# Late expert slots of one and a half blocks in place of two, with the two halves of the split in one matmul

## The chip, the core and the metric

The kernel runs on one core of one Trainium2 chip, as one program. The metric is the device time of one execution in microseconds. Before the change three runs gave 578.73, 578.89 and 579.51 us, so the median is 578.89 us.

## The reference, cut to what matters

The computation is an attention with a small memory, followed by a mixture of experts. The part that the change touches is the second one, for 4608 tokens of 512 numbers, 8 experts and 1024 hidden units:

```python
logits = x @ w_gate                      # x: 4608 x 512, from the attention
e_idx = np.argmax(logits, axis=1)        # one expert per token
probs = softmax(logits); gate_w = probs[arange(N), e_idx]
eom = 1.0 / (1.0 + np.exp(-(x @ w_output_gate)))
for e in range(8):
    mask = e_idx == e
    if not mask.any():
        continue
    h = np.maximum(x[mask] @ w1[e], 0.0)  # 512 -> 1024
    ye = h @ w2[e]                        # 1024 -> 512
    out[mask] = gate_w[mask, None] * eom[mask, e, None] * ye
```

With the inputs of this case the reference sends 576, 576, 0, 0, 576, 1152, 1152 and 576 tokens to the eight experts. These counts come from running the reference's routing, not from the trace.

## The kernel before, in words

The first 120 us belong mostly to the attention. It writes rows of `x` with their gate factor to a buffer `xs` in device memory, and the routing (`rank`, `route_early`, `route_late`) works out lists of token numbers for *slots*. A slot is one pass of one expert's 4 MB of weights over a fixed number of token blocks of 128. There are 5 early slots of three blocks, filled as soon as enough tokens are known, then 5 late slots of three (`NPT`), 4 late slots of two (`NPP`, below called pairs), and 22 single slots behind a branch, which run only if something is left over. `route_late` counts blocks per expert (`nbi`, L346 to L351), takes away triples, then makes a pair of every remainder of two blocks (L360), and leaves the rest to single slots. With the counts above, four experts have a remainder of two blocks, in each of which only 192 of the 256 places hold a token; no single slot runs.

The arithmetic keeps fp32 accuracy by splitting each operand into a first part (a cast to fp32r) and a second part (what the cast left over). A product is the sum of three matmuls: first x first, second x first, first x second (`PASS`). The layout of one slot, in `several`:

- Layer 1 has four steps `u`, each with one 512 KB piece of `w1`. In each of two halves `j` and four chunks `cc` of the 512 inputs there are three matmuls of moving width 128 times the number of blocks (L1176). The result stands in a PSUM bank; ScalarE writes `relu` of it as the first part `hh` (L1181), VectorE writes the second part `hl` (L1182). For a pair both halves share one bank and one such evacuation; for a triple each half has its own.
- Layer 2 has four steps `u` with pieces of `w2`, for each block `k` six matmuls of moving width 512 (L1198). After the last one `finish_y` scales the block with the gate on ScalarE (L1155) and scatters it to `out` with GpSimd (L1156). A result tile `y` has two buffers.

Each piece of weights is loaded by the SP queue (L553), cast by ScalarE (L564) and its second part subtracted by VectorE (L565). That is `split`; the finished halves go to a ring of ten places (`ring`, 2 + 2 + 6, grown by `GROW`). `done`, called after each step, moves the ring on: it issues at most two splits, and no more than nine pieces ahead of use (`ring.size - 1`), so that in the steady state each step issues exactly one. The tokens of a slot are gathered from `xs` by GpSimd, up to three slots ahead; for the slots behind the first late one (`quart`) this is done in quarters of 32 tokens, four indirect DMAs for each block (L519). `turn_x` then transposes a chunk on VectorE (L1035), casts it on ScalarE (L1043) and subtracts on VectorE (L1044). It is called for the four chunks of the *next* slot during layer 2 of the current one (`TURN`).

The order is written out by hand: every engine executes its instructions in the order in which the program lists them, and engines wait for each other by semaphores. What ScalarE and VectorE find in their queues during a slot is therefore this, in this order: in layer 1, for each `u`, the evacuations and then one split (cast, subtraction); in layer 2 the `turn_x` chunks of the next slot with the splits between them; and `finish_y` behind the chunks. The PSUM pool of this stage has six banks that are used in turn.

Of the kernel before, what the change touches and what calls it, by code (L numbers as in the profile page):

```python
# [16 lines left out]
P = 128  # L17
# [49 lines left out]
def attention_moe(tc, phiT, kv, qT, wgo, wall, out):  # L67
# [3 lines left out]
    with contextlib.ExitStack() as ctx:  # L71
# [266 lines left out]
        def route_late():  # L338
# [4 lines left out]
            yield from hold(LATE["dve"])  # L343
            epc = epcs[-1]
            nbi = rt.tile([P, E], I32, name="nbi", bufs=1)
            V.tensor_scalar(nbi[:], n_, 127.0, None, ALU.add)  # L346
            taken.clear()
            yield
            V.tensor_scalar(nbi[:], nbi[:], 7, None, ALU.arith_shift_right)
# [8 lines left out]
            V.tensor_tensor(ti[:, 2], nbi[:], ti[:, 0], ALU.subtract)  # L358
            yield
            V.tensor_scalar(ti[:, 1], ti[:, 2], 2.0, 2.0, ALU.is_ge, ALU.mult)  # L360
            yield
            V.tensor_tensor(ti[:, 2], ti[:, 2], ti[:, 1], ALU.subtract)
            yield
# [134 lines left out]
        for s in range(NSLOT):  # L498
# [4 lines left out]
            else:  # L503
# [3 lines left out]
            slots.append({"s": s, "nb": nb, "q0": q0, "idx": idx[nm], "rows": rows,  # L507
                          "nm": nm, "quart": s not in WHOLE,
                          "known": False, "listed": False})
        order = slots  # L510

        def gather(z):
            z["xg"] = xgs.tile()
            for k in range(z["nb"]):
                q = z["q0"] + k
                if z["quart"]:
                    rows = 4 * z["rows"]
                    for b in range(4):
                        G.indirect_dma_start(  # L519
                            out=z["xg"][:, k, XQ * b:XQ * b + XQ], out_offset=None,  # L520
                            in_=xs[0:z["rows"]].rearrange("t (a q) -> (t a) q", a=4),
                            in_offset=bass.IndirectOffsetOnAxis(ap=z["idx"][2][:, b, q:q + 1], axis=0),
                            bounds_check=rows - 1, oob_is_err=False)
                    continue
                G.indirect_dma_start(
                    out=z["xg"][:, k], out_offset=None, in_=xs[0:z["rows"]],
                    in_offset=bass.IndirectOffsetOnAxis(ap=z["idx"][0][:, q:q + 1], axis=0),
                    bounds_check=z["rows"] - 1, oob_is_err=False)
# [492 lines left out]
        def turn_x(z, c):  # L1021


            nb, xg = z["nb"], z["xg"]
            n = nb * P
            if c == 0:
                z["x"] = (mo.tile([P, 4, 3 * P], F32R, name="xh"), mo.tile([P, 4, 3 * P], F32R, name="xl"))
                if z["quart"]:
                    z["g"] = env["xt"].tile([P, 3], F32, name="gx")
                    for b in range(4):  # L1030
                        A.copy(z["g"][32 * b:32 * b + 32, 0:nb], xg[0:32, 0:nb, XQ * b + P])
            xh, xl = z["x"]
            if z["quart"]:
                xt = env["xt"].tile([P, 3 * P], F32, name="xt")
                V.transpose(xt[:, 0:n].rearrange("p (k i) -> p k i", i=32),  # L1035
                            xg[:, 0:nb].rearrange("p k (b q) -> p (k b) q", b=4)[:, :, 32 * c:32 * c + 32])
                pt = xt[:, 0:n]
            else:
                pt = bank([512], "ps")
                for k in range(nb):  # L1040
                    T.transpose(pt[:, k * P:(k + 1) * P], xg[:, k, c * XQ:c * XQ + P], ident[:])
                pt = pt[:, 0:n]
            A.copy(xh[:, c, 0:n], pt)  # L1043
            V.tensor_tensor(xl[:, c, 0:n], pt, xh[:, c, 0:n].bitcast(F32), ALU.subtract)  # L1044

        NT = 5 * NBP
        deferred = []
# [104 lines left out]

        def finish_y(z, k, py):
            y = mo.tile([P, DM], F32, name="y", bufs=2)
            A.activation(y[:], py, AF.Copy, scale=z["g"][:, k:k + 1] if z["quart"] else z["xg"][:, k, P:P + 1])  # L1155
            G.indirect_dma_start(  # L1156
                out=out, out_offset=bass.IndirectOffsetOnAxis(ap=z["idx"][1][:, z["q0"] + k:z["q0"] + k + 1], axis=0),
                in_=y[:], in_offset=None, bounds_check=NTOK - 1, oob_is_err=False)

        def several(i, st, nxt, hook):  # L1160

            z = order[i]
            nb, x, h = z["nb"], z["x"], []
            n_ = nb * P
            for u in range(4):
                w = st.take(i, u)
                h_ = mo.tile([P, 2, 3 * P], F32R, name="hh", bufs=4)
                l_ = mo.tile([P, 2, 3 * P], F32R, name="hl", bufs=4)
                for j in range(2):
                    if nb == 3 or j == 0:  # L1170
                        pb = bank([1, 512] if nb == 3 else [2, 256], "ps")
                    n = 0
                    for cc in range(4):
                        for a, b in PASS:
                            o = cc * 256 + j * P
                            T.matmul(pb[:, j % pb.shape[1], 0:n_], w[:, b, o:o + P], x[a][:, cc, 0:n_],  # L1176
                                     start=(n == 0), stop=(n == 11))
                            n += 1
                    if nb == 3 or j == 1:
                        js = slice(j, j + 1) if nb == 3 else slice(0, 2)  # L1180
                        A.activation(h_[:, js, 0:n_], pb[:, :, 0:n_], AF.Relu)  # L1181
                        V.scalar_tensor_tensor(l_[:, js, 0:n_], pb[:, :, 0:n_], 0.0, h_[:, js, 0:n_].bitcast(F32),  # L1182
                                               ALU.max, ALU.subtract)
# [6 lines left out]

            turns = [(u, k) for u in range(4, 8) for k in range(nb)]
            if 8 * i + 8 == st.hi:
                turns.sort(key=lambda t: t[1])
            for step, (u, k) in enumerate(turns):
                w = st.take(i, u)
                for f in range(2):
                    for n, (a, b) in enumerate(PASS):
                        T.matmul(py[k], h[u - 4][a][:, f, k * P:(k + 1) * P], w[:, b, DM * f:DM * f + DM],  # L1198
                                 start=(u == 4 and f == 0 and n == 0), stop=(u == 7 and f == 1 and n == 2))
# [5 lines left out]
                if k == nb - 1:  # L1205
                    st.done(PUMP[0])

        def single(i, st, nxt):
# [157 lines left out]
```

## Time and profile before

| | us |
|---|---|
| median of three runs | 578.89 |
| time of the profiled execution | 577.36 |
| span of the profiled execution | 575.6 |
| TensorE matmul busy | 529.1 (92%) |
| VectorE busy | 356.1 (62%) |
| ScalarE busy | 280.4 (49%) |
| GpSimd busy | 229.2 (40%) |
| mean granted clock | 0.966 |

The late slots stand at the end of the span. By the timeline the last four late triples start at 345.1, 378.0, 411.1 and 444.1 us, the four pairs at 477.1, 499.5, 522.0 and 544.4 us, and the last matmul starts at 566.6 us. The columns of the profile are busy time, number of instructions, and mean nanoseconds of one. Matmuls overlap in it: the mean length of one is its latency, and the distance between two starts is what it costs.

### The profile page before, as it was taken

The numbers are of one execution on the slowest core, as the hardware profiler recorded it, in microseconds if no ns is written. First come the engines' busy times: TensorE is split into PE (matmuls) and PEld (weight loads), VectorE is DVE, ScalarE is ACT, GpSimd is POOL, SyncE is SP. The second block draws the span as 40 slices with busy tenths as digits, with TensorE's granted clock in tenths as the row PEclk, the third lists the DMA queues.
The fourth block names the chain that finished last, engine by engine and source line by source line (L and its number), as shares of the span: only waits on it lengthen the run. The fifth ranks groups of instructions, "written<-read, shape, count | busy, mean of one in ns | idle before, by whom it ended". The sixth has DMA issues, their size and how long they took to land. (4 is left out here: it accounts for less than half of the span.)

```text
span 575.6 us, 10886 instructions
## 1 busy us (share of the span) xinstructions
PE 529.1 (92%) x4031; PEld 455.6 (79%) x4031; DVE 356.1 (62%) x736; ACT 280.4 (49%) x496; POOL 229.2 (40%) x253
## 2 busy tenths in 40 slices
PE   3688886789899999999999999999999999999993
PEld 2455554478689799898998989898998989899893
DVE  4485979767765659996443555646465555676610
ACT  3475655454254456453434545445454445656510
POOL 2242575831166034312471735547170604553011
PEclk9987879989899999999999999999999999999998
DMA  8999999975367659756564665656465655687000
GB/s 308 413 401 391 382 376 356 308 301 168 116 197 245 209 173 308 246 155 183 161 200 145 204 177 180 184 171 176 139 202 168 179 172 181 198 264 223 7 28 32
DMA packets 42238, 124.14 MB, mean 216 GB/s; under 512 B 10368, under 2 KB 10432, under 8 KB 41792
## 3 DMA queue, kind: packets, MB, share of 16 engines
q1 hardware_dynamic: 35136, 102.71, 54.7%
q0 software_dynamic: 7040, 20.65, 10.4%
q8 instruction: 33, 0.54, 0.4%
q14 instruction: 29, 0.24, 0.1%
HBM read 102.99 MB, written 20.87 MB: 215 GB/s over the span
## 5 line engine op out<-in xcount | busy, mean ns | idle before, releaser
L1176 PE MATMUL bps<-xh,whl 128*128 128x384 f32 (+1 forms) x896 | 213.6, 322 | 0.1
L1198 PE MATMUL bps<-whl,hh 128*128 128x512 f32 x608 | 197.7, 396 | 0.0
L565 DVE TENSOR_TENSOR whl<-w,whl 128x1024 fp32r<-128x1024 f32 x112 | 136.8, 1228 | 68.5 <-ACT whl L564 68.5
L1176 PEld LDWEIGHTS bps<-xh,whl 128*128 128x128 f32 x896 | 156.9, 190 | 1.9 <-issue 0.6
L1176 PE MATMUL bps<-xl,whl 128*128 128x384 f32 (+1 forms) x448 | 143.8, 321 | 0.0
L1198 PEld LDWEIGHTS bps<-whl,hh 128*128 128x128 f32 x608 | 114.7, 189 | 26.1 <-issue 2.5
L1198 PE MATMUL bps<-whl,hl 128*128 128x512 f32 x304 | 119.0, 391 | 0.0
L564 ACT CAST whl<-w 128x1024 fp32r<-128x1024 f32 x112 | 116.4, 1046 | 0.0
L519 POOL DMA_INDIRECT xg<-xs,idx_ql x80 | 90.2, 1127 | 25.2 <-issue 24.3
L1181 ACT ACTIVATE hh<-bps 128x384 fp32r<-128x384 f32 (+1 forms) x96 | 48.9, 510 | 96.9 <-PE bps L1176 96.7
L1182 DVE SCALAR_TENSOR_TENSOR hl<-bps,hh 128x384 fp32r<-128x384 f32 (+1 forms) x96 | 55.1, 577 | 52.1 <-ACT hh L1181 52.1
L1176 PEld LDWEIGHTS bps<-xl,whl 128*128 128x128 f32 x448 | 85.1, 190 | 0.5
L1156 POOL DMA_INDIRECT out<-y,idx_ol x23 | 24.9, 1081 | 127.1 <-ACT y L1155 101.4
L1198 PEld LDWEIGHTS bps<-whl,hl 128*128 128x128 f32 x304 | 57.5, 189 | 10.8
L838 POOL TENSOR_TENSOR ea<-ea,mx 128x512 f32<-128x512 f32 (+1 forms) x20 | 19.2, 961 | 49.8 <-DVE mx L836 45.4
L1043 ACT CAST xh<-xt 128x384 fp32r<-128x384 f32 (+1 forms) x32 | 14.7, 460 | 37.9 <-DVE xt L1035 37.9
L873 ACT COPY xo<-bpd 128x576 f32<-128x576 f32 x36 | 22.6, 640 | 21.3 <-PE bpd L871 12.7
L956 POOL TENSOR_SCALAR Aw<-iota_row,row 128x128 bf16<-128x128 bf16 x36 | 26.8, 759 | 12.4 <-DVE row L946 12.4
L871 PE MATMUL bpd<-ve_b,aT 64*128 64x144 f32 (+1 forms) x320 | 28.5, 327 | 2.4 <-DVE ea L833 2.4
L1044 DVE TENSOR_TENSOR xl<-xt,xh 128x384 fp32r<-128x384 f32 (+1 forms) x32 | 15.8, 492 | 24.1 <-ACT xh L1043 24.1
L1155 ACT ACTIVATE y<-bps,gx 128x512 f32<-128x512 f32 x20 | 13.4, 687 | 30.4 <-PE bps L1198 13.9
L871 PEld LDWEIGHTS bpd<-ve_b,aT 64*128 64x128 f32 (+1 forms) x320 | 21.7, 196 | 8.1 <-issue 3.5
(248 smaller groups left out, 471.6 us busy)
## 6 DMA issues: line engine op xcount, KB each, us to landing
w<-wall SPq DMA_DIRECT2D x112, 512.0 KB, 3.9
kvt<-kv SPq DMA_DIRECT2D x32, 512.0 KB, 7.5
xs<-xo SPq DMA_DIRECT2D x16, 576.0 KB, 5.8
qt<-qT SPq DMA_DIRECT2D x16, 512.0 KB, 9.1
ph<-phiT SPq DMA_DIRECT2D x3, 1152.0 KB, 12.1
kv<-kv SPq DMA_DIRECT2D x4, 512.0 KB, 9.0
xg<-xs,idx_ql POOLq DMA_INDIRECT x80, 4.2
ph<-phiT SPq DMA_DIRECT2D x4, 288.0 KB, 3.2
```

What stands on the lines that cost most here:

```text
L519: G.indirect_dma_start(out=z["xg"][:, k, XQ * b:XQ * b + XQ], out_offset=None, in_=xs[0:z["rows"]].rearrange("t (a q) -> (t a) q", a=4), i ...
L564: A.copy(hl[:, 0], w[:])
L565: V.tensor_tensor(hl[:, 1], w[:], hl[:, 0].bitcast(F32), ALU.subtract)
L838: G.tensor_tensor(eav, eav, mx[:, 0:n].unsqueeze(2).to_broadcast([P, n, M]), ALU.subtract)
L871: T.matmul(px[to:to + n, r, sl], z["aT"][h, o:o + n], ves[2 * bp + b][h, g], start=True, stop=True)
L873: A.copy(xo[:, c % 2], px[:, :, 0:2 * XQ])
L956: (G if AWP else V).tensor_scalar(Aw[:, bp * NCH + c], iota_row[:], row[:, c:c + 1], None, ALU.is_equal)
L1156: G.indirect_dma_start(out=out, out_offset=bass.IndirectOffsetOnAxis(ap=z["idx"][1][:, z["q0"] + k:z["q0"] + k + 1], axis=0), in_=y[:], in ...
L1176: T.matmul(pb[:, j % pb.shape[1], 0:n_], w[:, b, o:o + P], x[a][:, cc, 0:n_], start=(n == 0), stop=(n == 11))
L1181: A.activation(h_[:, js, 0:n_], pb[:, :, 0:n_], AF.Relu)
L1182: V.scalar_tensor_tensor(l_[:, js, 0:n_], pb[:, :, 0:n_], 0.0, h_[:, js, 0:n_].bitcast(F32), ALU.max, ALU.subtract)
L1198: T.matmul(py[k], h[u - 4][a][:, f, k * P:(k + 1) * P], w[:, b, DM * f:DM * f + DM], start=(u == 4 and f == 0 and n == 0), stop=(u == 7 an ...
```

## The change

The four pairs become slots of one and a half blocks, 192 tokens, and stand between the triples.

- Routing: a flag `odd` says whether the expert's number of half blocks is odd. Only a remainder of two blocks whose second is at most half full becomes a pair. Three VectorE instructions on 128 x 8 numbers are added, with one more step in the routing's generator.
- `x` of a pair: first and second part lie next to each other in one tile of 384 columns. The second block is gathered with two indirect DMAs in place of four, and `turn_x` works on 192 columns.
- Layer 1 of a pair: for each `j` and `cc` one matmul with the first part of the weights over all 384 columns, and one with the second part over 256 columns, in place of three over 256. Each `j` now has a bank of its own. The two sums of columns have to be added: ScalarE copies the second 192 columns out of PSUM, VectorE adds the first, ScalarE writes `relu`, VectorE subtracts twice (64 and 128 columns), so that first and second part of the half block lie next to each other.
- Layer 2 of a pair: six matmuls for the whole block as before; for the half block four, since its first and second parts are the 128 stationary columns of one matmul. `finish_y` of that block copies the lower 64 rows (ScalarE), adds the upper ones (VectorE), then scales and scatters 64 rows.
- Order: T0, T1, P0, T2, P1, T3, P2, T4, P3, where T are the late triples and P the pairs. In the last slot the half block is done first.
- The ring of split weights has nine places in place of ten.

```diff
-GROW = ((2, 2, 2), (6, 1, 0))
+GROW = ((2, 2, 2), (5, 1, 0))
...
+            V.tensor_scalar(odd[:], n_, 63.0, None, ALU.add)
...
+            V.tensor_scalar(odd[:], odd[:], 6, 1, ALU.arith_shift_right, ALU.bitwise_and)
...
+            V.tensor_tensor(ti[:, 1], ti[:, 1], odd[:], ALU.mult)
...
-        order = slots
+        a, b = NPE + NPT, NPE + NPT + NPP
+        order = slots[:NPE + 1]
+        for s in range(max(NPT - 1, NPP)):
+            order += slots[NPE + 1 + s:a][:1] + slots[a + s:b][:1]
+        order += slots[b:]
...
-                    for b in range(4):
+                    for b in range(2 if (z["nb"], k) == (2, 1) else 4):
...
-            V.tensor_tensor(xl[:, c, 0:n], pt, xh[:, c, 0:n].bitcast(F32), ALU.subtract)
+            lo = xh[:, c, n:2 * n] if nb == 2 else xl[:, c, 0:n]
+            V.tensor_tensor(lo, pt, xh[:, c, 0:n].bitcast(F32), ALU.subtract)
...
+            if (z["nb"], k) == (2, 1):
+                n = 64
+                ya = env["xt"].tile([64, DM], F32, name="ya", bufs=1)
+                A.copy(ya[:], py[64:128])
+                V.tensor_tensor(ya[:], py[0:64], ya[:], ALU.add)
+                py = ya[:]
...
+                        elif cc < 3:
+                            T.matmul(pb, wh, x[0][:, cc], start=(cc == 0), stop=False)
+                            T.matmul(pb[:, 0:256], wl, x[0][:, cc, 0:256], start=False, stop=False)
...
+                        s_ = env["xt"].tile([P, 192], F32, name="hsum")
+                        A.copy(s_[:], pb[:, 192:384])
+                        V.tensor_tensor(s_[:], pb[:, 0:192], s_[:], ALU.add)
+                        A.activation(h_[:, j, 0:192], s_[:], AF.Relu)
+                        for o, c, n in ((192, P, 64), (256, 0, P)):
+                            V.scalar_tensor_tensor(h_[:, j, o:o + n], s_[:, c:c + n], 0.0,
+                                                   h_[:, j, c:c + n].bitcast(F32), ALU.max, ALU.subtract)
...
-                turns.sort(key=lambda t: t[1])
+                turns.sort(key=lambda t: t[1], reverse=nb == 2)
...
+                    elif k == 0:
+                        ps = [(h_[:, f, 256 * a:256 * a + P], b) for a, b in PASS]
+                    else:
+                        ps = [(h_[:, f, P:256], b) for b in range(2)]
```

More of the change, by code (lines that the diff above doesn't have):

```diff
@@ L360, in route_late @@
             V.tensor_scalar(ti[:, 1], ti[:, 2], 2.0, 2.0, ALU.is_ge, ALU.mult)
+            yield
+            V.tensor_tensor(ti[:, 1], ti[:, 1], odd[:], ALU.mult)
             yield
@@ L1024, in turn_x @@
             nb, xg = z["nb"], z["xg"]
-            n = nb * P
+            n = 192 if nb == 2 else nb * P
             if c == 0:
-                z["x"] = (mo.tile([P, 4, 3 * P], F32R, name="xh"), mo.tile([P, 4, 3 * P], F32R, name="xl"))
+                z["x"] = (mo.tile([P, 4, 3 * P], F32R, name="xh"), mo.tile([P, 4, 3 * P], F32R, name="xl") if nb != 2 else None)
                 if z["quart"]:
@@ L1030, in turn_x @@
                     for b in range(4):
-                        A.copy(z["g"][32 * b:32 * b + 32, 0:nb], xg[0:32, 0:nb, XQ * b + P])
+                        m = 1 if nb == 2 and b > 1 else nb
+                        A.copy(z["g"][32 * b:32 * b + 32, 0:m], xg[0:32, 0:m, XQ * b + P])
             xh, xl = z["x"]
@@ L1167, in several @@
                 h_ = mo.tile([P, 2, 3 * P], F32R, name="hh", bufs=4)
-                l_ = mo.tile([P, 2, 3 * P], F32R, name="hl", bufs=4)
+                l_ = mo.tile([P, 2, 3 * P], F32R, name="hl", bufs=4) if nb == 3 else None
                 for j in range(2):
-                    if nb == 3 or j == 0:
-                        pb = bank([1, 512] if nb == 3 else [2, 256], "ps")
-                    n = 0
+                    pb = bank([512], "ps")[:, 0:3 * P]
                     for cc in range(4):
[L1174 to L1183, printed above, removed]
+                        o = cc * 256 + j * P
+                        wh, wl = w[:, 0, o:o + P], w[:, 1, o:o + P]
+                        if nb == 3:
+                            T.matmul(pb, wh, x[0][:, cc], start=(cc == 0), stop=False)
+                            T.matmul(pb, wh, x[1][:, cc], start=False, stop=False)
+                            T.matmul(pb, wl, x[0][:, cc], start=False, stop=(cc == 3))
+                        elif cc < 3:
+                            T.matmul(pb, wh, x[0][:, cc], start=(cc == 0), stop=False)
+                            T.matmul(pb[:, 0:256], wl, x[0][:, cc, 0:256], start=False, stop=False)
+                        else:
+                            T.matmul(pb[:, 0:256], wl, x[0][:, cc, 0:256], start=False, stop=False)
+                            T.matmul(pb, wh, x[0][:, cc], start=False, stop=True)
+                    if nb == 3:
+                        A.activation(h_[:, j], pb, AF.Relu)
+                        V.scalar_tensor_tensor(l_[:, j], pb, 0.0, h_[:, j].bitcast(F32), ALU.max, ALU.subtract)
+                    else:
+                        s_ = env["xt"].tile([P, 192], F32, name="hsum")
[5 more added lines that the diff above has]
+                                                   h_[:, j, c:c + n].bitcast(F32), ALU.max, ALU.subtract)
@@ L1196, in several @@
                 for f in range(2):
-                    for n, (a, b) in enumerate(PASS):
-                        T.matmul(py[k], h[u - 4][a][:, f, k * P:(k + 1) * P], w[:, b, DM * f:DM * f + DM],
-                                 start=(u == 4 and f == 0 and n == 0), stop=(u == 7 and f == 1 and n == 2))
+                    h_, l_ = h[u - 4]
+                    if nb == 3:
+                        ps = [((h_, l_)[a][:, f, k * P:(k + 1) * P], b) for a, b in PASS]
+                    elif k == 0:
+                        ps = [(h_[:, f, 256 * a:256 * a + P], b) for a, b in PASS]
+                    else:
+                        ps = [(h_[:, f, P:256], b) for b in range(2)]
+                    for n, (a, b) in enumerate(ps):
+                        T.matmul(py[k], a, w[:, b, DM * f:DM * f + DM],
+                                 start=(u == 4 and f == 0 and n == 0),
+                                 stop=(u == 7 and f == 1 and n == len(ps) - 1))
                 if u == 7:
@@ L1204, in several @@
                     nxt(TURN[nb].index(step))
-                if k == nb - 1:
+                if (step + 1) % nb == 0:
                     st.done(PUMP[0])
```

11 lines of the change are left out of this document (6 added, 5 removed).

## The prediction

> **What bounds the kernel now.** I read the page first, then the busy time slot by slot, then the order of the instructions on each engine around one pair. The page gives the span and the busiest engine:
>
> ```profile
> span 575.6 us, 10886 instructions
> PE 529.1 (92%) x4031; PEld 455.6 (79%) x4031; DVE 356.1 (62%) x736; ACT 280.4 (49%) x496; POOL 229.2 (40%) x253
> ```
>
> The average hides the stage that the change touches. These are the last triple and the first pair, each one slot long (columns: stretch, its length, busy time of TensorE, of its weight loads, VectorE, ScalarE, GpSimd, then granted clock and DMA):
>
> ```profile
> 444.10:477.10 33.00, 33.00 (x169) 30.17 (x168) 17.05 (x24) 15.65 (x27) 11.61 (x11) 1.00 0.56 169
> 477.10:499.50 22.40, 22.40 (x145) 20.52 (x144) 13.86 (x18) 11.78 (x20) 11.88 (x10) 1.00 0.67 208
> ```
>
> TensorE never pauses, so here its instructions set the time, and all else is cover. In the pair VectorE is busy 13.86 of 22.40 us. What a matmul costs is the distance between starts, read where the kinds change (a triple from 378.04, a pair from 477.12):
>
> ```profile
> 378.04 0.33 PE L1176 MATMUL bps<-xh,whl 128*128 128x384 f32 x1
> ...
> 394.70 0.39 PE L1198 MATMUL bps<-whl,hh 128*128 128x512 f32 x1
> ...
> 411.06 0.33 PE L1176 MATMUL bps<-xh,whl 128*128 128x384 f32 x1
> ...
> 477.12 0.28 PE L1176 MATMUL bps<-xh,whl 128*128 128x256 f32 x1
> ...
> 488.63 0.40 PE L1198 MATMUL bps<-whl,hh 128*128 128x512 f32 x1
> ...
> 499.54 0.28 PE L1176 MATMUL bps<-xh,whl 128*128 128x256 f32 x1
> ```
>
> A triple has 96 matmuls of width 384 in 16.66 us (0.1735 each) and 72 of 512 in 16.36 us (0.227); a pair 96 of 256 in 11.51 us (0.120) and 48 of 512 in 10.91 us (0.227). Triple 33.02 us, pair 22.42 us.
>
> **The change on TensorE.** A pair will have 32 matmuls of width 384, 32 of 256 and 40 of 512: 5.55 + 3.84 + 9.09 = 18.48 us. That takes 3.94 us off each pair, 15.8 us off four, if the cover holds. The rest of the sum asks whether it holds.
>
> **The change on ScalarE and VectorE.** Durations, by form:
>
> ```profile
> L565 DVE TENSOR_TENSOR whl<-w,whl 128x1024 fp32r<-128x1024 f32 x112 | 136.8, 1228 | 68.5 <-ACT whl L564 68.5
> ...
> L564 ACT CAST whl<-w 128x1024 fp32r<-128x1024 f32 x112 | 116.4, 1046 | 0.0
> ...
> L1035 DVE STREAM_TRANSPOSE xt<-xg 128x384 f32<-128x384 f32 x16 | 9.1, 572 | 0.0
> L1044 DVE TENSOR_TENSOR xl<-xt,xh 128x384 fp32r<-128x384 f32 x16 | 8.9, 559 | 14.4 <-ACT xh L1043 14.4
> L1043 ACT CAST xh<-xt 128x384 fp32r<-128x384 f32 x16 | 8.2, 513 | 18.5 <-DVE xt L1035 18.5
> ...
> L1044 DVE TENSOR_TENSOR xl<-xt,xh 128x256 fp32r<-128x256 f32 x16 | 6.8, 426 | 9.7 <-ACT xh L1043 9.7
> L1043 ACT CAST xh<-xt 128x256 fp32r<-128x256 f32 x16 | 6.5, 407 | 19.4 <-DVE xt L1035 19.4
> ```
>
> The new widths are not in the trace. On the line through 256 and 384 columns VectorE takes 0.36 us for 192, 0.295 for 128 and 0.23 for 64; ScalarE 0.35 for 192. Bounds: in proportion to the columns, 0.32 on VectorE for 192, 0.21 and 0.11 (no fixed part); as long as the 256-column row, 0.43 each. I take the line, since both its ends are rows and the 0.69 of 512 columns below lies on it too. How instructions follow each other, on VectorE and ScalarE:
>
> ```profile
> 478.43 0.69 ACT L1155 ACTIVATE y<-bps,gx 128x512 f32<-128x512 f32 x1 [1.79 <-DMA out<-y,idx_ol]
> ...
> 492.01 0.41 ACT L1043 CAST xh<-xt 128x256 fp32r<-128x256 f32 x1 [0.91 <-DVE xt L1035]
> ```
> ```profile
> 480.09 1.23 DVE L565 TENSOR_TENSOR whl<-w,whl 128x1024 fp32r<-128x1024 f32 x1 [4.06 <-ACT whl L564]
> 481.24 0.69 DVE L1182 SCALAR_TENSOR_TENSOR hl<-bps,hh 128x512 fp32r<-128x512 f32 x1
> ...
> 492.45 0.42 DVE L1044 TENSOR_TENSOR xl<-xt,xh 128x256 fp32r<-128x256 f32 x1 [0.47 <-ACT xh L1043]
> ```
>
> Behind an unrelated instruction the next one starts 0.08 us before its end (481.24 against 480.09 + 1.23; I use 0.09); behind the other engine's result 0.03 us after it (492.45 against 492.42). Now the queue of one `u` of layer 1, from the end of the previous `u`'s last relu as zero:
>
> - ScalarE casts the next weight piece: -0.09 to 0.96. VectorE subtracts it: 0.99 to 2.22.
> - First `j`: copy out of PSUM behind the cast, done at 1.22; VectorE's add must stand behind the weight subtraction, 2.13 to 2.49; relu to 2.87; the two subtractions to 3.34 (0.23 + 0.295 - 0.09 behind a 0.03 wait).
> - Second `j`: its copy runs under that; add 3.25 to 3.61, relu to 3.99, its subtractions later, under the next cast.
>
> So ScalarE and VectorE hand each `j` back and forth three times and need 3.95 us for a `u` for which TensorE now needs 2.35 (8 x 0.1735 + 8 x 0.120). Before, a `u` of a pair had one relu and one subtraction, and 2.88 us of matmuls to hide them. The busy time of both engines stays under the slot's length; it is the order that costs.
>
> From the slot's start S: the triple in front leaves a result tile waiting for a DMA (the row at 478.43, S + 1.3), then a cast and a subtraction, so VectorE is free for the first add at 481.24, S + 4.12. The last relu of the `u` then ends at S + 5.98, 9.93, 13.88 and 17.83, and the parts that layer 2 reads are complete 0.47 us after each. Layer 1 takes TensorE 9.39 us; the six banks suffice (the seventh use of a bank, at S + 7.0, needs the first add, done at 4.48; the eighth, at 8.2, the second, done at 5.60). Layer 2 takes 2.27 us per `u`: the third waits from 13.93 to 14.38, the fourth from 16.65 to 18.33, the slot's matmuls end at S + 20.6. Two of the 3.94 us are gone.
>
> What is late next is worse. Behind the layer-1 work both queues hold the four `turn_x` chunks of the next slot, which now is a triple. Their pitch with a weight split between them is in the rows of the triple that precedes a triple:
>
> ```profile
> 431.68 0.56 DVE L1044 TENSOR_TENSOR xl<-xt,xh 128x384 fp32r<-128x384 f32 x1 [0.58 <-ACT xh L1043]
> ...
> 434.93 0.56 DVE L1044 TENSOR_TENSOR xl<-xt,xh 128x384 fp32r<-128x384 f32 x1 [0.58 <-ACT xh L1043]
> ```
>
> 3.25 us. The fourth split of layer 1 ends at 17.83 + 2.22 = S + 20.05. The first chunk is then transposed, cast and subtracted (0.57, 0.51, 0.56 and two waits) by 21.66, the second by 24.91, the third by 28.16, the fourth, with no split in front, by 29.77. The triple's first sum of matmuls needs all four; TensorE could have started it at 20.6 and gets through it at 29.80 + 0.52 = 30.32. Seven more such sums (84 x 0.1735) and layer 2 (16.36) end at S + 61.25. Before, pair and triple took 22.42 + 33.02 = 55.44. So each of the three pairs with a triple behind it costs 5.8 us: +17.4. The triple itself catches up: its queues have 33 us for 17 us of work.
>
> P3 has nothing behind it and no weights left to split. Without the split a `j` needs 0.36 + 0.35 + 0.435 + 0.06 - 0.09 = 1.12 us on the chain, under TensorE's 1.17, so it only carries the late start: its last parts are ready at S + 13.1, where TensorE, the half block done first, wants them at 12.1. It ends at about 19.5 instead of 22.42: -2.9. Sum so far +14.5 us.
>
> **The clock.** TensorE has 7.6 us with about a fifth of its work in front of each of three triples. Earlier stretches show what the clock does then (same columns):
>
> ```profile
> 108.00:112.00 4.00, 1.41 (x39) 0.61 (x30) 3.04 (x8) 1.22 (x4) 3.67 (x5) 1.00 0.95 318
> 112.00:116.00 4.00, 4.00 (x52) 2.40 (x52) 1.93 (x6) 3.32 (x8) 2.15 (x3) 0.63 1.02 414
> ...
> 96.00:100.00 4.00, 2.57 (x63) 1.72 (x61) 3.96 (x28) 2.98 (x6) 2.35 (x4) 1.00 1.01 390
> ...
> 28.00:32.00 4.00, 1.31 (x5) 1.02 (x6) 3.85 (x8) 3.44 (x10) 1.07 (x2) 0.50 0.99 400
> 32.00:36.00 4.00, 4.00 (x44) 2.27 (x46) 3.40 (x9) 2.81 (x7) 2.46 (x5) 0.69 1.03 406
> ```
>
> Behind a stretch with a third of its work, four full microseconds ran at 0.63 and 0.69: 1.5 and 1.2 us lost. With 2.57 of 4 busy nothing was lost. I take 1.5 us for each stall, 4.5 in all; ends 0 and 3 each. The Trainium skill, "TensorE: Matmul & The Clock Gate", part 1, says that the clock halves only after a whole idle window of about 3.4 us. By that rule, with 2.7 us at most between the triple's chunks, the clock would hold, and the sum would stay at +14.5; the stretch from 108 to 112, busy 1.41 of 4 us and followed by 0.63, speaks for the other.
>
> **What costs nothing.** GpSimd issues eight gathers less, routing has three short instructions and one step more, the ring one place less:
>
> ```profile
> L519 POOL DMA_INDIRECT xg<-xs,idx_ql x80 | 90.2, 1127 | 25.2 <-issue 24.3 <-DMA xg<-xs,idx_ql 0.6 <-DVE hl L1182 0.3
> ```
> ```profile
> L525 POOL DMA_INDIRECT xg<-xs,idx_gl x3: 1016/1057/1440, 266.8 to 269.5; - x3
> ```
> ```profile
> L349 DVE TENSOR_SCALAR nbi<-nbi x1: 228/228/228, 205.2 to 205.2; 128x8 int32<-128x8 int32 x1
> ```
> ```profile
> L1041 PE MATMUL bps<-ident,xg x12: 270/272/273, 296.9 to 309.1; 128*128 128x128 f32 x12
> ```
>
> Gathers: 8 x 1.13 us on an engine busy 11.9 of 22.4. Routing: 3 x 0.23 us near 205, and the lists are used for the gathers at 266.8 whose rows are first turned at 296.9, so some 25 us lie between; if that cover were gone, about 1 us. Eight pieces ahead are still one whole slot, so every weight a slot needs is split in the slot before. The half block's extra copy and add in `finish_y` stand behind the fourth chunk and in front of nothing that TensorE waits for, since the next triple's banks have been free since layer 1. The end of the span (last scatter) is the same.
>
> **The sum.** 577.36 us of the profiled execution + 14.5 + 4.5 = 596.4. The median of the runs lies 1.5 us above that execution, so I expect 597.9 us. The bounds of the new widths: in proportion, a `u` needs about 3.6 us, the fourth chunk comes 1.4 us earlier, and the sum falls by 4.2 to 593.7; at 0.43 for each it needs about 4.5, and the sum rises by 6.6 us to 604.5.
>
> **The rivals.**
>
> 1. *The clock holds.* Everything as above without the 4.5 us: 593.4. For it the row at 96; against it those at 108 and 28.
> 2. *The clock falls twice*, in the fourth `u`'s wait and at the triple, 3 us a time: 578.9 + 14.5 + 9 = 602.4.
> 3. *TensorE stays the bound* (other side). If VectorE could add and subtract under the weight splits, a `u` would need its busy time alone, 2 x 0.885 + 1.23 = 3.0 us, or less; from a fourth chunk at S + 23.9 (55.44 - 16.36 - 14.57 - 0.55) a pair is no longer slower, which is 5.9 us earlier than I work out. With no wait left: 578.9 - 15.8 = 563.1. For it: busy time per pair, some 20 us on VectorE, fits in the 55 us of pair and triple. Against it: the order is fixed, and the rows at 480 and 481 show VectorE taking them in it, one behind the other.
> 4. *Pairs turn into single slots*, because a remainder is over 192. Two singles of 48 matmuls of 256 and 24 of 512 cost 2 x 11.2 us, so well over 610. The reference sends exactly 576 or 1152 tokens to each expert in use, so 192 remain.
>
> **Chances.** Forecast 0.45, rival 1 0.22, rival 2 0.17, rival 3 in full or in part (down to no loss) 0.14, rival 4 0.02. A difference under about 0.2% (1.2 us) can't be told from none. Faster 0.12, within 0.2% 0.03 (both from rival 3 and cases beside it), slower 0.85. The likeliest case's own range is 593.5 to 603. The range for 8 in 10 holds rivals 1 and 2 and the bounds of the widths: 588 to 604.5.
>
> **What would show it.** In the trace after: TensorE waiting about 7.6 us at the start of each triple behind a pair, released by VectorE's subtraction for `x` (L1044's successor); a wait of 1.7 us in the fourth `u` of layer 2, released by `h`; VectorE's first add 4.1 us into the pair and adds 3.95 us apart per `u`; granted clock under 1 behind the stalls. The prediction is wrong if T2 starts its layer 1 without a wait, or if the pitch per `u` is near 2.4 us.

## The result, and the profile after

The changed kernel takes 597.02 us (median of four runs, 595.63 to 599.36), the kernel before 578.93 us in the same comparison. The ratio is 1.0315, with a 95% interval of 1.0281 to 1.0348, so the change costs about 18 us. (Here and below medians are of all runs and ratios of the fast runs alone, so a ratio need not be the quotient of two medians.) The profiled execution took 596.88 us, with a mean granted clock of 0.943 (before 0.966).

Slot by slot, read from the first matmul of each slot in the timeline of TensorE (us; T are the late triples, P the pairs, in the order in which they run):

| | T0, T1 | P0 + T2 | P1 + T3 | P2 + T4 | P3 |
|---|---|---|---|---|---|
| before (a pair and a triple) | 33.03, 33.03 | 55.44 | 55.44 | 55.44 | 22.58 |
| after | 33.02, 33.03 | 62.22 | 63.43 | 62.52 | 19.51 |
| forecast | same | 61.25 + 1.5 | 61.25 + 1.5 | 61.25 + 1.5 | 19.5 |

The three pairs and the triples behind them lose 6.8, 8.0 and 7.1 us, together 21.9; the last pair gains 3.1. Two pieces lie outside these slots: the first late triple starts 1.75 us later than before, and the end of the span comes 1.1 us nearer to the last matmul. Together 21.9 - 3.1 + 1.75 - 1.1 = 19.45 us, which is the difference of the two spans (595.1 and 575.6).

The page after. TensorE has 160 matmuls less than before, yet 3 us more of busy time (532.2 against 529.1). Of these, 1.9 us lie ahead of the late slots (276.1 against 274.2) and 1.2 in them (256.1 against 255.0), where the granted clock is 0.96 instead of 1.00 and a matmul at half clock takes longer. The slices are 14.9 us long; they show a dip at the start of each of the three triples behind a pair, with a lower granted clock in the same slice:

```profile
span 595.1 us, 10687 instructions
PE 532.2 (89%) x3871; PEld 448.0 (75%) x3871; DVE 369.8 (62%) x823; ACT 290.7 (49%) x548; POOL 216.5 (36%) x245
PE   3688777698999999999999999987999699959994
PEclk9878878889899999999999999997999699989999
```

VectorE and ScalarE are busy for the same shares of the span as before, 62% and 49%. The busy shares therefore say nothing of what went wrong. The stretches of the first pair, of the triple behind it and of the last pair do (same columns as in the prediction):

```profile
379.79:401.07 21.28, 19.61 (x106) 16.55 (x104) 12.20 (x31) 11.21 (x28) 8.02 (x8) 1.00 0.55 160
401.07:442.01 40.94, 36.95 (x168) 31.66 (x169) 24.42 (x35) 20.86 (x35) 16.65 (x15) 0.92 0.64 185
...
567.96:587.47 19.51, 19.12 (x105) 16.56 (x103) 7.46 (x26) 7.61 (x20) 2.86 (x3) 1.00 0.15 49
```

The triple's stretch is 7.9 us longer than the 33.03 of before, with the same 168 matmuls. What TensorE and its weight loads wait for in the late slots (columns: engine, tile, line, what released it; total us, times, longest); in the kernel before, no such wait on ScalarE or VectorE appears there:

```profile
PEld bps L1197 <- ACT xh L1055: 19.9, 12, 2.4
PE bps L1197 <- ACT xh L1055: 14.7, 9, 2.0
PEld bps L1198 <- DVE xl L1058: 4.2, 12, 0.4
PEld bps L1239 <- ACT hh L1214: 4.0, 6, 1.0
```

Twelve waits, which are three triples by four chunks: L1197 is the first matmul of a triple's chunk, and it waits for the cast of `x` that `turn_x` makes. VectorE's timeline from the start of P0 at S = 379.79 shows why that cast comes late:

```profile
382.81 1.22 DVE L576 TENSOR_TENSOR whl<-w,whl 128x1024 fp32r<-128x1024 f32 x1 [4.13 <-ACT whl L575]
383.95 0.35 DVE L1213 TENSOR_TENSOR hsum<-bps,hsum 128x192 f32<-128x192 f32 x1
...
387.93 0.35 DVE L1213 TENSOR_TENSOR hsum<-bps,hsum 128x192 f32<-128x192 f32 x1
...
391.93 0.35 DVE L1213 TENSOR_TENSOR hsum<-bps,hsum 128x192 f32<-128x192 f32 x1
...
395.92 0.35 DVE L1213 TENSOR_TENSOR hsum<-bps,hsum 128x192 f32<-128x192 f32 x1
...
401.05 0.56 DVE L1058 TENSOR_TENSOR xl<-xt,xh 128x384 fp32r<-128x384 f32 x1 [0.58 <-ACT xh L1055]
...
404.29 0.56 DVE L1058 TENSOR_TENSOR xl<-xt,xh 128x384 fp32r<-128x384 f32 x1 [0.58 <-ACT xh L1055]
...
407.53 0.56 DVE L1058 TENSOR_TENSOR xl<-xt,xh 128x384 fp32r<-128x384 f32 x1 [0.58 <-ACT xh L1055]
...
409.15 0.56 DVE L1058 TENSOR_TENSOR xl<-xt,xh 128x384 fp32r<-128x384 f32 x1 [0.58 <-ACT xh L1055]
```

The first adds of two successive `u` lie 3.99 us apart (383.95, 387.93, 391.93, 395.92), although TensorE needs only 2.35 us for a `u`. Only then come the chunks, 3.24 us apart (the fourth, with no split in front of it, 1.62). TensorE follows them one for one:

```profile
396.71 3.25 PE L1239 MATMUL bps<-whl,hh 128*128 128x512 f32 x10 [0.57 <-ACT hh L1214]
401.07 0.45 PE L1197 MATMUL bps<-xh,whl 128*128 128x384 f32 x1 [1.10 <-ACT xh L1055]
...
404.31 0.44 PE L1197 MATMUL bps<-xh,whl 128*128 128x384 f32 x1 [2.03 <-ACT xh L1055]
...
407.55 0.69 PE L1197 MATMUL bps<-xh,whl 128*128 128x384 f32 x1 [1.64 <-ACT xh L1055]
...
409.17 0.69 PE L1197 MATMUL bps<-xh,whl 128*128 128x384 f32 x1
...
410.57 0.52 PE L1197 MATMUL bps<-xh,whl 128*128 128x384 f32 x1
410.89 0.52 PE L1198 MATMUL bps<-xl,whl 128*128 128x384 f32 x1
```

### The profile page after: what moved, and what is told of

Its sections match the earlier page's. It is cut to its first block, busy times and chain, and to the rows that moved or that the text cites. A ratio compares the mean times of both kernels' runs of the same rounds, so it can differ in the third digit from the quotient of the medians.

```text
span 595.1 us, 10687 instructions
## 1 busy us (share of the span) xinstructions
PE 532.2 (89%) x3871; PEld 448.0 (75%) x3871; DVE 369.8 (62%) x823; ACT 290.7 (49%) x548; POOL 216.5 (36%) x245
## 5 line engine op out<-in xcount | busy, mean ns | idle before, releaser
L1239 PE MATMUL bps<-whl,hh 128*128 128x512 f32 x640 | 198.5, 399 | 2.1 <-ACT hh L1214 1.7
L1239 PEld LDWEIGHTS bps<-whl,hh 128*128 128x128 f32 x640 | 120.2, 189 | 33.0 <-ACT hh L1214 4.0
L1197 PE MATMUL bps<-xh,whl 128*128 128x384 f32 x320 | 112.9, 353 | 14.8 <-ACT xh L1055 14.7
L1198 PE MATMUL bps<-xl,whl 128*128 128x384 f32 x320 | 112.3, 351 | 0.8 <-DVE xl L1058 0.5
L1199 PE MATMUL bps<-xh,whl 128*128 128x384 f32 x320 | 110.3, 345 | 0.0
L1239 PE MATMUL bps<-whl,hl 128*128 128x512 f32 x240 | 94.2, 392 | 0.0
L530 POOL DMA_INDIRECT xg<-xs,idx_ql x72 | 77.5, 1076 | 21.9 <-issue 20.1
L1197 PEld LDWEIGHTS bps<-xh,whl 128*128 128x128 f32 x320 | 62.6, 196 | 21.0 <-ACT xh L1055 19.9
L1207 ACT ACTIVATE hh<-bps 128x384 fp32r<-128x384 f32 x80 | 39.0, 492 | 72.3 <-PE bps L1199 72.2
L1208 DVE SCALAR_TENSOR_TENSOR hl<-bps,hh 128x384 fp32r<-128x384 f32 x80 | 43.9, 553 | 37.4 <-ACT hh L1207 37.1
L1198 PEld LDWEIGHTS bps<-xl,whl 128*128 128x128 f32 x320 | 62.4, 195 | 4.4 <-DVE xl L1058 4.2
L1199 PEld LDWEIGHTS bps<-xh,whl 128*128 128x128 f32 x320 | 62.7, 196 | 0.0
L1239 PEld LDWEIGHTS bps<-whl,hl 128*128 128x128 f32 x240 | 45.5, 190 | 8.3
L1201 PE MATMUL bps<-xh,whl 128*128 128x384 f32 x96 | 29.5, 338 | 0.0
```

Source lines behind the costliest of these rows:

```text
L530: G.indirect_dma_start(out=z["xg"][:, k, XQ * b:XQ * b + XQ], out_offset=None, in_=xs[0:z["rows"]].rearrange("t (a q) -> (t a) q", a=4), i ...
L1197: T.matmul(pb, wh, x[0][:, cc], start=(cc == 0), stop=False)
L1198: T.matmul(pb, wh, x[1][:, cc], start=False, stop=False)
L1199: T.matmul(pb, wl, x[0][:, cc], start=False, stop=(cc == 3))
L1201: T.matmul(pb, wh, x[0][:, cc], start=(cc == 0), stop=False)
L1207: A.activation(h_[:, j], pb, AF.Relu)
```

## The experiments

The theory was that each instruction costs little, and that the order in which ScalarE and VectorE must take them costs the time: the weight split stands between the evacuations of a pair, and the next triple's chunks stand behind all of it. The rivals: the order of slots does it; the copy and the add do it by their own length; TensorE or the clock does it. Lengths of slots below are read from the first matmuls, as above. Each group of runs has its own runs of the kernel before, whose medians were 578.73 to 578.94 us.

**Only the order of the slots and the smaller ring, on the kernel before.**

```diff
-GROW = ((2, 2, 2), (6, 1, 0))
+GROW = ((2, 2, 2), (5, 1, 0))
-        order = slots
+        a, b = NPE + NPT, NPE + NPT + NPP
+        order = slots[:NPE + 1]
+        for s in range(max(NPT - 1, NPP)):
+            order += slots[NPE + 1 + s:a][:1] + slots[a + s:b][:1]
+        order += slots[b:]
```

> The kernel before with only the order of the slots (triples and pairs by turns) and the ring of nine places; pairs keep two whole blocks and three matmuls of width 256. Hand-over theory (what costs is ScalarE and VectorE handing each half of layer 1 back and forth in the pairs): a pair is as long as before, 22.4 us, and the fourth chunk of the triple behind it comes about 0.3 us late, three times: 579.8 us (578.5 to 581.5). Rival, order and ring: the turns or the ninth ring place cost the 18 us, so 590 us or more.

Measured 580.98 us, ratio 1.0039 (1.0010 to 1.0069). Pairs took 22.42 us as before, the triples behind them 33.63, 33.65 and 33.69 instead of 33.03. The waits of weight loads in the late slots:

```profile
PEld bps L1181 <- DVE xl L1049: 1.2, 3, 0.4
PEld bps L1181 <- ACT xh L1048: 0.7, 3, 0.3
```

Running triples behind pairs costs 0.6 us each, 1.9 in all. The other 16 us need the narrower pair.

**All slots of three first, on the changed kernel.** The opposite edit: the new pairs, in the old order.

```diff
-        a, b = NPE + NPT, NPE + NPT + NPP
-        order = slots[:NPE + 1]
-        ...
+        order = slots
```

> The changed kernel with the slots in the old order, all triples, then the four pairs. Hand-over theory: a pair behind a pair waits for its chunks (6.4 us, a little less than a triple since they are narrower), then for banks and for h, three times, and P3 starts late too: 578.9 + 16.7 + 4.5 for the clock = 600 us (596 to 605). Rival, the order by turns is what costs: 580 us or less.

Measured 596.6 us, ratio 1.0284 (1.0231 to 1.0336), the same as the change within its spread. The four pairs now take 21.38, 29.25, 29.27 and 27.18 us. The second pair, in the columns used above:

```profile
501.66:530.91 29.25, 22.75 (x104) 18.80 (x105) 18.60 (x41) 16.18 (x36) 8.45 (x8) 0.88 0.61 173
```

The largest wait of TensorE in the four pairs is again the one for the chunks of `x`:

```profile
PE bps L1197 <- DVE xh L1054: 17.1, 9, 2.3
```

VectorE is busy 18.60 of 29.25 us and ScalarE 16.18, and still together they set the length, with a granted clock of 0.88 on top. Every pair behind a pair pays here for the chain of the pair in front of it, and no triple catches up. So turns are neither the cause nor a cure: 107.08 us for four pairs against 89.84 before is +17.2, by the same chain and the clock behind it. Two of the triples took 33.97 and 33.93 us, each behind a scatter that took 5.4 and 5.5 us to land; whether the one follows from the other was not tried.

**The weight splits of a pair later.** Layer 1 of a pair issues no split, layer 2 one for each step, and the triple makes up for the rest.

```diff
-                st.done(PUMP[0])
+                st.done(PUMP[0] if nb == 3 else 0)
...
-                    st.done(PUMP[0])
+                    st.done(PUMP[0] if nb == 3 else 1)
```

> The changed kernel, but a pair's layer 1 issues no weight split and its layer 2 one per step; the triple behind it makes up with two per step. The same instructions in all, only later in the queues. Hand-over theory: without the split a half of layer 1 needs 1.12 us on the chain, under the 1.17 us of its matmuls, so a pair ends after 18.5 us and the wait at the next triple falls from 7.6 to about 2.8 us: 572 us (569 to 577). Rival, plain load (VectorE and ScalarE have too much work per pair wherever it stands): no gain, 595 us or more.

Measured 579.61 us, ratio 1.0023 (0.9987 to 1.0060). Moving a cast and a subtraction gives back 17 of the 18 us, without one instruction less. Pairs took 18.46 us, which is the forecast of 18.48 for TensorE alone. But the triples behind them took 39.38, 36.26 and 36.05 us, the first of them far over what was expected, and the time lies 2.6 us above the expected range. These lengths are those of the profiled execution, which took 575.84 us, 3.8 less than the median; what the other executions wait for stands in no trace. ScalarE, around the start of P0 at 380.24:

```profile
377.77 0.69 ACT L1177 ACTIVATE y<-bps,gx 128x512 f32<-128x512 f32 x1 [0.51 <-ACT whl L575]
...
379.13 0.69 ACT L1177 ACTIVATE y<-bps,gx 128x512 f32<-128x512 f32 x1
383.59 0.69 ACT L1177 ACTIVATE y<-bps,gx 128x512 f32<-128x512 f32 x1 [3.78 <-DMA out<-y,idx_ol]
```

The third result tile of the triple in front takes the buffer of the first, and must wait until that one's scatter has landed. ScalarE stands still for 3.78 us, and everything behind it in its queue with it. In the kernel after the same instruction starts at 381.15, S + 1.36; here at S + 3.35. The expectation had taken this date as fixed, and that is a part of the miss.

**Without the copy and the add.** This kernel leaves out the second part of `x` times the first part of `w1` in the pairs: `relu` and the subtractions read the first 192 columns of the bank directly.

```diff
-                        s_ = env["xt"].tile([P, 192], F32, name="hsum")
-                        A.copy(s_[:], pb[:, 192:384])
-                        V.tensor_tensor(s_[:], pb[:, 0:192], s_[:], ALU.add)
-                        A.activation(h_[:, j, 0:192], s_[:], AF.Relu)
+                        s_ = pb
+                        A.activation(h_[:, j, 0:192], s_[:, 0:192], AF.Relu)
```

> The changed kernel without the copy and the add in a pair's layer 1: relu and the two subtractions read the first 192 columns of the bank straight away. It leaves out the product of the second part of x with the first part of the first-layer weights in the four pairs. TensorE does the same work, the weight splits stand where they stood. Hand-over theory: a step of layer 1 then needs about 2.9 us or less on the chain and the next triple waits 1.9 us in place of 7.6: 568.6 us (566 to 573). Rival, the splits alone (the add is harmless): 590 us or more. Rival, the clock alone: not much faster than 592 us.

Measured 572.41 us, ratio 0.9874 (0.9798 to 0.9951). VectorE in layer 1 of the first pair:

```profile
384.37 0.74 DVE L1214 SCALAR_TENSOR_TENSOR hh<-bps,hh 128x64 fp32r<-128x64 f32 x4
385.04 1.22 DVE L576 TENSOR_TENSOR whl<-w,whl 128x1024 fp32r<-128x1024 f32 x1
386.17 0.75 DVE L1214 SCALAR_TENSOR_TENSOR hh<-bps,hh 128x64 fp32r<-128x64 f32 x4
```

On VectorE a `u` takes 1.80 us in place of 3.99 (384.37 to 386.17). The add is only 2 x 0.35 us of the 2.19 saved. Nearly all of the rest is waiting between the two engines: with the add, VectorE stands idle for 0.51, 0.43 and 0.43 us in each `u` (386.79, 388.72 and 389.84 in the kernel after), since each `j` goes from ScalarE to VectorE and back, and its neighbour and the split must queue behind it; without it, there is no idle time in this stretch. Again the first two starts lay late by the result tile (ScalarE stood idle for 3.74 and 3.77 us until a landing), and the triples took 38.92, 37.58 and 34.84 us; the last one, with a shorter wait of 2.13, is close to the 33.0 + 1.9 = 34.9 that was expected.

**Sum in PSUM: three matmuls of 192 columns.** TensorE adds the parts itself; one relu and two subtractions serve both `j`.

```diff
-                        elif cc < 3:
-                            T.matmul(pb, wh, x[0][:, cc], start=(cc == 0), stop=False)
-                            T.matmul(pb[:, 0:256], wl, x[0][:, cc, 0:256], start=False, stop=False)
...
+                            T.matmul(pq[:, j], wh, x[0][:, cc, 0:192], start=(cc == 0), stop=False)
+                            T.matmul(pq[:, j], wh, x[1][:, cc, 0:192], start=False, stop=False)
+                            T.matmul(pq[:, j], wl, x[0][:, cc, 0:192], start=False, stop=(cc == 3))
```

> The changed kernel with three matmuls of width 192 in a pair's layer 1 in place of one of 384 and one of 256, so that TensorE adds the parts itself; both halves share a bank, with one relu and two subtractions for both; gather, layer 2 and order as in the change. What a matmul of width 192 costs stands in no trace so far. On the line through 256, 384 and 512 columns it is 0.093 us: then a pair takes 18.0 us, the next triple waits 2 us, 567.4 us (564 to 573). If it costs what 256 columns cost: 577.7 us. [...]

Measured 573.88 us, ratio 0.9888 (0.9848 to 0.9928), between the two prices and 0.9 us above the range of the first. TensorE at the start of the first pair, at full granted clock:

```profile
380.36 0.28 PE L1206 MATMUL bps<-xh,whl 128*128 128x192 f32 x1
380.47 0.27 PE L1204 MATMUL bps<-xh,whl 128*128 128x192 f32 x1
380.58 0.27 PE L1205 MATMUL bps<-xl,whl 128*128 128x192 f32 x1
```

A matmul of 192 columns costs 0.11 us, hardly less than the 0.120 of 256. The pairs took 19.80 to 19.98 us, which is 96 x 0.1115 + 40 x 0.227 = 19.8. The triples behind took 38.98, 37.05 and 35.11: the wait for the scatter again (the third activation starts at S + 3.50, 5.00 and 1.36). The profiled execution took 580.24 us, 6.4 above the median, so in the other executions these waits are probably shorter.

**Both causes at once.** The weight splits later, the chunks of the next slot one step earlier in each pair, and a result tile of its own for the third block of the late triples.

```diff
-TURN = {3: (1, 4, 6, 9), 2: (1, 2, 4, 5)}
+TURN = {3: (1, 4, 6, 9), 2: (0, 1, 2, 3)}
...
-            y = mo.tile([P, DM], F32, name="y", bufs=2)
+            y = env["xt"].tile([P, DM], F32, name="yx", bufs=1) if k == 2 and "xt" in env else mo.tile([P, DM], F32, name="y", bufs=2)
...
-                st.done(PUMP[0])
+                st.done(PUMP[0] if nb == 3 else 0)
...
-                    st.done(PUMP[0])
+                    st.done(PUMP[0] if nb == 3 else 1)
```

> The late split of e2, and two more moves: the four chunks of the next slot are turned in the first four steps of a pair's layer 2 in place of steps 1, 2, 4 and 5, and the third block of a late triple has a result tile of its own, so that ScalarE does not wait for the scatter of the first at the start of the pair. Arithmetic, order and ring as in the change. Hand-over theory: both queues are then done with the next triple's chunks before the pair ends; no wait is left, a pair takes 18.5 us and the triple behind it 33.0: 563.1 us (561 to 567). Rival, plain load: VectorE has some 20 us of work in a pair of 18.5 us, so the wait moves but stays, and the time is near e2's 579 us.

Measured 563.1 us (560.24 to 565.31), ratio 0.971 (0.9668 to 0.9753): faster than both kernels, and the price that the prediction's third rival gives for a TensorE that never waits. That the two agree to the tenth is luck: in the profiled execution (564.36 us) the slots behind T1 gain 15.1 of the 15.8 us, and T1 and the early part lose 1.5 and 1.7. First pair, first triple behind one and last pair (columns as above):

```profile
381.23:399.69 18.46, 18.46 (x106) 16.89 (x104) 10.98 (x32) 9.37 (x26) 7.72 (x8) 1.00 0.35 110
399.69:432.98 33.29, 33.29 (x170) 30.14 (x169) 24.56 (x34) 22.37 (x36) 19.57 (x16) 1.00 0.82 277
536.39:555.01 18.62, 18.62 (x105) 16.70 (x103) 7.47 (x26) 7.53 (x20) 3.88 (x3) 1.00 0.15 51
```

TensorE is busy for the whole of each stretch, at full clock. The triples took 33.29, 33.23 and 33.26 us. VectorE in layer 1 of the first pair:

```profile
384.28 0.35 DVE L1213 TENSOR_TENSOR hsum<-bps,hsum 128x192 f32<-128x192 f32 x1
...
385.41 0.35 DVE L1213 TENSOR_TENSOR hsum<-bps,hsum 128x192 f32<-128x192 f32 x1
...
386.53 0.35 DVE L1213 TENSOR_TENSOR hsum<-bps,hsum 128x192 f32<-128x192 f32 x1
```

Without a split between them, the adds are 1.125 us apart, 2.25 for a `u`, just under the 2.35 us of its matmuls. In this profile T1, the triple in front of the first pair, took 34.51 us instead of 33.03; why was not followed up.

**The same without the result tile, the tile alone on the changed kernel, and the tile alone on the kernel before.** These divide the gain.

```diff
-            y = mo.tile([P, DM], F32, name="y", bufs=2)
+            y = env["xt"].tile([P, DM], F32, name="yx", bufs=1) if k == 2 and "xt" in env else mo.tile([P, DM], F32, name="y", bufs=2)
```

> e5 without the result tile of its own. ScalarE stands at the start of each pair until a scatter has landed, some 2 to 3.5 us, and everything behind it comes later by that: 567 us if it stands 2 us (565 to 573). If the result tile does not matter, the same as e5.

> The changed kernel with nothing but the result tile of its own for the third block of a late triple. Hand-over theory: the pair's chain starts about 1.4 to 2 us earlier, the wait at the triple falls by as much, the rest stays: 592.5 us (590 to 595). Rival, the result tile is what the change lacked: 580 us or less.

> The kernel before, with nothing changed but a result tile of its own for the third block of the late slots that hold three (ring of streamed tiles 9 instead of 10). In the kernel before, the profile shows no matmul of a late slot that waits for ScalarE or VectorE, and its five slots of three are 33.03 us apart each, the rate of the matmuls. Theory (the tile gains time only where ScalarE's and VectorE's chain sets the pace): 578.9 us, slots of three still 33.0 us, slots of two still 22.4 us. Rival (the wait for the earlier scatter costs TensorE time in any order, so that 6.7 us of the best version's gain belong to the tile alone): 572 to 575 us.

| kernel | us | ratio, 95% interval | pairs in front of a triple | triples behind |
|---|---|---|---|---|
| splits later and chunks earlier, no tile | 569.79 | 0.983 (0.9779 to 0.9882) | 19.20, 18.46, 18.46 | 35.88, 34.46, 35.12 |
| changed kernel and tile | 591.94 | 1.0213 (1.0161 to 1.0266) | 20.17, 20.14, 20.14 | 41.39, 41.35, 41.31 |
| kernel before, tile and ring of nine | 578.56 | 0.9994 (0.9973 to 1.0015) | | |

In the kernel before, the tile is worth nothing (a pair and a triple still take 22.42 and 33.03 us there), since the chain of ScalarE and VectorE has slack. On the changed kernel it is worth 5.1 us, on the retimed one 6.7. Step by step from the change to the best version: splits later 597.0 to 579.6, chunks earlier to 569.8, the tile to 563.1. Splits later and chunks earlier both shorten the one queue; the tile takes the wait out of its head.

## Why the prediction was right, and where it was not

**TensorE alone.** 18.48 us was forecast for a pair; 18.46 was measured for ten pairs in the four versions in which nothing else set the pace. The pitches read from the kinds of matmuls were enough.

**The chain per `u`.** 3.95 us was forecast, 3.99 measured. The prediction's own list ends at 3.99, from relu to relu; the 3.95 that it went on with is a slip of 0.04 us, three times in front of the fourth `u`. The new widths, which had to be taken from a line through wider rows (columns: line, form, count; busy us, mean ns):

```profile
L1214 ACT ACTIVATE hh<-hsum 128x192 fp32r<-128x192 f32 x32 | 11.7, 364 | 27.9 <-DVE hsum L1213 27.9
L1213 DVE TENSOR_TENSOR hsum<-bps,hsum 128x192 f32<-128x192 f32 x32 | 11.2, 350 | 0.0
...
L1212 ACT COPY hsum<-bps 128x192 f32<-128x192 f32 x32 | 9.8, 306 | 0.0
...
L1216 DVE SCALAR_TENSOR_TENSOR hh<-hsum,hh 128x128 fp32r<-128x128 f32 x32 | 9.1, 284 | 0.0
...
L1216 DVE SCALAR_TENSOR_TENSOR hh<-hsum,hh 128x64 fp32r<-128x64 f32 x32 | 7.2, 225 | 13.8 <-ACT hh L1214 13.8
```

The add took 0.350 us (taken: 0.36), the subtractions 0.284 and 0.225 (0.295, 0.23), the relu 0.364 and the copy 0.306 (0.35 for both). Both bounds lay further off: in proportion to the columns 0.32, 0.21 and 0.11 for add and subtractions, or 0.43 for each. The first add stood at S + 4.16 (4.12).

**The wait inside layer 2.** The prediction's two waits of 0.45 and 1.7 us for `h` were mis-sized. P0's last matmul ends at 401.07 - 1.10 = 399.97, S + 20.2, where 20.6 was forecast, and the end of a matmul in the profile lies 0.39 us behind its start where the forecast counted a pitch of 0.23, so about 0.6 of 2.15 us was not there. A `u` of layer 2 may begin with the half `j` = 0, which is ready 1.1 us before the other (L1239 at 396.71 starts 0.05 us behind the relu of that half, which ends at 396.66); the forecast made it wait for both. It changed nothing, since the triple had to wait for its chunks anyway. The sign that was named, a wait of 1.7 us in the fourth `u`, is 0.57 us in the profile; the rest is spread over small delays of the matmuls around it.

**The triple's chunks.** The fourth chunk was forecast for S + 29.77 and is done at 409.71, S + 29.92; in the other two triples at S + 29.88 and S + 29.92. This one date sets the loss; the slip of 3 x 0.04 us explains most of the 0.15. Two signs were named less well. The releaser is mainly the cast (14.7 us of TensorE's waits in the three triples) and hardly the subtraction (0.5), because the first matmul of a chunk needs only the first part of `x`. And TensorE stands idle for 5.1 us of each triple, where the forecast had 7.6; the two count differently, since the profile takes a matmul as busy for its whole latency (0.44 to 0.69 us in the rows from 401.07 to 409.17) and the forecast for 0.1735.

**The clock.** 62.22, 63.43 and 62.52 us are 0.97, 2.18 and 1.27 above the 61.25 without a clock term, 4.4 together, where 4.5 was forecast. Some 0.4 of it is the chunks' 0.15 us each; what is left, 4.0, stands in the rows. Behind the stalls matmuls of 384 columns follow each other 0.32 us apart (410.57 and 410.89 above) where 0.1735 is the full rate. The granted clock (third column from the end) around the first and the second triple:

```profile
400.00:402.00 2.00, 0.79 (x3) 0.48 (x3) 1.03 (x3) 1.46 (x2) 0.00 (x0) 1.00 0.48 82
402.00:404.00 2.00, 0.28 (x2) 0.00 (x0) 1.71 (x2) 0.26 (x1) 0.00 (x0) 1.00 0.45 180
404.00:406.00 2.00, 1.45 (x3) 0.69 (x3) 1.32 (x2) 1.20 (x2) 0.00 (x0) 0.71 0.82 225
406.00:408.00 2.00, 0.45 (x1) 0.29 (x1) 1.42 (x3) 0.51 (x1) 0.00 (x0) 0.50 0.45 76
408.00:410.00 2.00, 1.97 (x5) 1.02 (x5) 1.13 (x3) 1.39 (x3) 0.00 (x0) 0.50 0.59 223
...
412.00:414.00 2.00, 2.00 (x13) 2.00 (x12) 0.29 (x1) 1.97 (x3) 0.21 (x1) 1.00 0.82 133
...
474.00:476.00 2.00, 2.00 (x8) 2.00 (x8) 0.28 (x2) 1.78 (x3) 0.41 (x1) 0.50 0.72 119
```

The second triple still ran at half clock 4 us after its last chunk, the first for 2. This refutes rival 1, that the clock holds. The Trainium skill, "TensorE: Matmul & The Clock Gate", part 1, lets the clock fall after a whole idle window of some 3.4 us; here no wait was longer than 2.4 us, a few matmuls lay between any two of them, and the clock fell to 0.50. By these rows the measurement decides against the rule as it was applied. Rival 2 (a fall in the pair as well, 3 us for each) is refuted too: the pair's stretch has a granted clock of 1.00.

**The last pair.** 19.51 us, forecast about 19.5. The term of -2.9 is -3.1 against P3's own 22.58.

**What was to cost nothing.** No single slot ran (rival 4): the nine late slots fill the stretch up to the end. The early part is 1.75 us longer. The first late triple started between 311.06 and 313.40 us in three profiles with the old routing and between 312.2 and 314.19 in eight with the new one; means of 312.2 and 313.6, so a part may belong to the routing, and it stays open. The end of the span was said to be the same and is not: from the end of P3's slot to the end of the span the kernel before needs 8.7 us (8.7 to 8.8 in the three kernels with its pairs), the changed one 7.6 (7.6 to 8.0 in the eight with the new ones). In both, the last scatter is issued about 1 us behind the last matmul, so the microsecond lies behind that issue; why was not tried.

**The time itself.** 597.9 us forecast, 597.0 measured. That is closer than its parts deserve. The slots gave 18.8 us where 19.0 were summed, the early part and the end, both left out, add 0.7, and the 1.5 us by which the median lay above the profiled execution before are 0.1 after.

**Rival 3 and the step that the experiments found weak.** That TensorE stays the bound was refuted for this order of instructions, and its price of 563.1 us is what a better order reaches. The busy time was right on what could be hidden; the order decided that it wasn't. The step with a hidden weakness was "a result tile waiting for a DMA (the row at 478.43, S + 1.3)". It was taken as a fixed date, and in the changed kernel it held (S + 1.36 in P0). But it is the landing of a scatter. From the issue to the release of the third activation 2.9 us passed after (378.29 to 381.15), 4.9 us with the later splits (378.73 to 383.59). The profile of the kernel before had shown that the date is not fixed. At the starts of its five slots behind late triples the third activation stands at S + 1.37, 1.39, 3.14, 1.33 and 1.31; the third is this row, with S = 411.06 and the scatter issued at 409.51:

```profile
414.20 0.69 ACT L1155 ACTIVATE y<-bps,gx 128x512 f32<-128x512 f32 x1 [3.61 <-DMA out<-y,idx_ol]
```

It cost nothing there (the triple still takes 33.03 us), and the prediction read only the last of the five. That the date held in all three pairs of the changed kernel that stand in front of a triple (S + 1.36, 1.32 and 1.36) is luck, since the prediction gave no reason for it. The expectations of three kernels were off by it: in all three the head of the first pair's queue was late by 2 more microseconds, in two of them that of the second pair by 3.6, and the triples behind these pairs took 1.9 to 4.1 us more than the last triple of the same version.

## What to carry to other kernels

When an edit makes TensorE faster, redo the dates of the engines that evacuate for it and prepare its next operands, in the order of their queues: here ScalarE and VectorE were busy for 49% and 62% of the span before and after, and lost 18 us by standing in line for each other. Work with a distant due date (a weight split for the next slot) does not belong between the links of a chain that hands data back and forth; moving it gave back 17 us with the same instructions. A buffer that waits for a DMA at the head of an engine's queue delays all that follows by a time that varies; it costs nothing as long as the queue has slack, so ask again once the slack is gone.

## What the runs showed of the hardware

- A matmul with 128 stationary columns costs 0.1115 us for 192 moving columns and 0.120 for 256, but 0.1735 for 384 and 0.227 for 512. From 256 columns on, 128 more cost 0.0535 us; from 256 to 192 only 0.0085 is saved. Three matmuls of 192 columns save less than their columns promise, and one of 384 for two of 192 saves 0.05 us.
- The granted clock fell from 1.00 to 0.50 with TensorE working now and then (0.79 and 0.28 of 2 us in the first two rows above) and no single wait over 2.4 us, and it stayed at 0.50 for 2.0, 4.6 and 2.6 us after the last chunk of the three triples was ready.
- The landing of an indirect scatter of 128 rows that another result tile waits for took 2.8 to 5.5 us from its issue, at the same place of nearly the same program: 2.8 at its shortest (544.85 to 547.67 without copy and add), 5.0 in the retimed version without the tile (378.29 to 383.30), 5.5 at its longest (413.78 to 419.27 with all slots of three first). What makes it vary was not tried.
